# Recurrence and gated feed-forward on one core: two inputs turned by DMA transposes, and a new order for the first 900 jobs

## Chip, cores and metric

One core of a Trainium2 chip runs the whole program. The metric is device time in microseconds (us); smaller is better. TensorE (PE) does matrix products and turns tiles with an identity matrix, VectorE (DVE), ScalarE (ACT) and GpSimd (POOL) work element by element, and SyncE (SP) issues the DMAs, one queue for all of them.

## The reference

Four sequences of 5824 tokens with 256 channels pass a gated linear recurrence, and then a feed-forward block that multiplies two projections. In short:

```python
a_base = 1 / (1 + exp(-a_param))                  # [256]
a_t = exp(8 * sigmoid(r_gate) * log(clip(a_base)))
x_gated = sqrt(max(1 - a_t*a_t, 1e-6)) * sigmoid(i_gate) * x
for t in range(S):
    h = a_t[:, t] * h + x_gated[:, t]             # the scan over time
    y[:, t] = h
tok = y.reshape(23296, 256)
out = ((tok @ w1) * (tok @ w2)) @ w3 @ w_out      # 256 -> 1024 -> 1024 -> 256
```

## The kernel before

The 23296 tokens are cut into 47 chunks: chunks 0 and 1 have 256 tokens, chunks 2 to 45 have 512, chunk 46 has 256. Chunks 0 and 1 share their tiles up to the scan. Since nothing stands between the last two products, w3 and w_out are first folded into one 1024 x 256 matrix `wp_sb`, in eight pieces.

The program is a list of small jobs. Each is a letter with a chunk number and further indices, and one long string, `ORDER`, gives their sequence; each engine works through its own jobs in that sequence and waits wherever an input or a free buffer is missing. For a chunk c the jobs are:

- `r`, `i`, `x`: loads of r_gate, i_gate and x, tokens on the partitions. `Lw..` and `Cw..` load a piece of a weight and cast it to bf16.
- `R`, `I` (ACT): tanh of half the gates. `p` (POOL) adds 1 to the i gate. `t` multiplies it with x into `u_t`, in two halves, on POOL, or on DVE for the entries of `DV_HALF`.
- `V` turns `th_r`, and `U` turns `u_t`, from tokens on partitions to channels on partitions. For chunks in `TURN_R` or `TURN_U` this is done by `turn_pe`: eight 128x128 transposes on PE into a PSUM tile `ptr`. For the others `turn_dma` issues one DMA transpose on SP into a tile `rt` or `ut`.
- `d` (ACT) takes the exponential: `a_t`. `s` squares it into `nrm` (POOL, or ACT for `AC_SQUARE`, DVE for `DV_SQUARE`), `q` (ACT) takes the square root, `g` (DVE) multiplies by the turned `u_t`, `h` (DVE) scans, one instruction for each half of the channels, `y` casts the result to bf16 (POOL unless named elsewhere). A tile `y_t` is what PE needs to begin on a chunk.
- `a` and `b` (PE) are the projections by w1 into `pa` and by w2 into `pb`; `c` copies `pa` out of PSUM into `sa` (ACT, or DVE for `DV_COPY`), `m` (DVE) multiplies `sa` by `pb` into `g_t`.
- `D` (PE) multiplies `g_t` by `wp_sb` into `po`, `e` evacuates it into `ot` (ACT, or DVE for `DV_EVAC`), `o` stores.
- `Ft`, `Fc`, `Fm`, `Fe` fold w3 with w_out: PE transposes into `ptw`, a copy into `w3t`, PE products into `pw`, a scaled copy into `wp_sb`.
- `W` (PE) are products of the identity with itself. They compute nothing; they stand where PE would have nothing else to do at the start.

The tiles `ptr`, `pa`, `po`, `ptw` and `pw` share one ring of four PSUM buffers, taken in the order of the program; `pb` and the tiles of `W` share a ring of two. So a `pa` can be written only when the fourth tile before it has been read. `u_t` has two buffers, `ut` six.

A chunk in both `TURN_R` and `TURN_U` is loaded in long rows: each partition takes four neighbouring tokens, 4 KB in one piece, and the later jobs reorder them. Any other chunk is loaded with 1 KB rows. The two ways of turning, and that rule, are:

```python
def long_rows(c):
    return c in TURN_R and c in TURN_U

def turn_pe(c, key, nm, half=None):            # shortened: one matmul for each 128x128 block
    nc.tensor.matmul(out=pt[:, cb - cbs[0], j * P:(j + 1) * P],
                     lhsT=flat(T[nm, c])[:, j, cb * P:(cb + 1) * P], rhs=ident, is_transpose=True, ...)

def turn_dma(c, key, nm):
    ...
    nc.sync.dma_start_transpose(out=dense(dst, n).rearrange("p cb j q -> p (cb j) q"),
                                in_=dense(T[nm, c], n).rearrange("p cb j q -> p (cb j q)"))
```

The line numbers in the rows below: 155 load, 196 product into `u_t`, 204 PE turn, 215 DMA transpose, 227 exponential, 235 and 237 square, 242 root, 252 and 255 the product `g`, 274 scan, 284 and 286 cast to `y_t`, 291 `W`, 303 projections, 324 and 326 PSUM copies, 341 product `m`, 361 down product, 418 and 420 weight casts, 429 and 440 folding products, 474 and 476 the scaled copy. In the changed kernel each number is two lower.

## Time and profile before

| | |
|---|---|
| median of 3 runs | 510.43 us (510.37 to 511.27) |
| the profiled execution | 510.6 us, of which 508.8 us from the first to the last instruction |
| PE busy | 497.0 us, 98% |
| DVE, ACT, POOL busy | 445.7, 452.2, 299.9 us |
| DMA moved | 124.32 MB, mean 244 GB/s |

Busy time says that an instruction was in progress. Matmuls overlap one another, so the pace of PE is read from the starts of neighbouring rows, and whether it stands still from the waits.

### The profile page before, as it was taken

How to read it: one execution, taken by the hardware profiler on the slowest of the kernel's cores; microseconds unless marked ns; L12 is line 12 of the kernel's file. 1: busy time of each engine (PE TensorE's matmuls, PEld its weight loads, DVE VectorE, ACT ScalarE, POOL GpSimd, SP SyncE). 2: the span in 40 equal slices, each digit the busy share in tenths (PEclk: the TensorE clock that was granted, in tenths of full speed). 3: DMA queues.
4: the chain of work that ended last, by engine and by line, in shares of the span. 5: the costliest groups of instructions: out<-in, count | busy, mean ns of one | idle time of the engine just before them, and what ended most of it. 6: DMA issues, size and time to landing. Idle time of an engine off the chain costs nothing.

```text
span 508.8 us, 8833 instructions
## 1 busy us (share of the span) xinstructions
PE 497.0 (98%) x3162; PEld 307.4 (60%) x3217; DVE 445.7 (88%) x450; ACT 452.2 (89%) x683; POOL 299.9 (59%) x261
## 2 busy tenths in 40 slices
...
GB/s 319 399 369 338 261 270 330 289 268 273 310 294 272 241 274 283 321 266 293 242 278 337 252 268 195 220 238 227 208 248 152 240 316 146 89 167 62 64 52 104
DMA packets 179104, 124.32 MB, mean 244 GB/s; under 512 B 88434, under 2 KB 175092, under 8 KB 179060
## 3 DMA queue, kind: packets, MB, share of 16 engines
...
## 4 chain that ended last, share of the span: by engine, by line
PE 85%; ACT 6%; DMA 3%; issue 3%; DVE 2%; POOL 1%; SPq 0%; DVEq 0%; ACTq 0%; POOLq 0%
PE po L361 28%; PE pb L303 27%; PE pa L303 26%; ACT sa L326 2%; DMA x_t<-in_x_dram 2%; PE pw L440 1%; ACT a_t L227 1%; DMA i_t<-in_i_gate_dram 1%; PE ptr L204 1%; DVE h_t L274 1%; ACT ot L326 1%; PE ptw L429 1%; ACT L172 1%; ACT nrm L242 0%; ACT th_r L166 0%
## 5 line engine op out<-in xcount | busy, mean ns | idle before, releaser
L341 DVE TENSOR_TENSOR g_t<-sa,pb 128x1024 bf16<-128x1024 bf16 (+1 forms) x188 | 217.9, 1178 | 44.4 <-PE pb L303 21.6
L303 PEld LDWEIGHTS <-w_sb 128*128 128x128 bf16 x1504 | 146.4, 98 | 146.0 <-POOL w_sb L420 1.6
L326 ACT CAST sa<-pa 128x512 bf16<-128x512 f32 (+1 forms) x311 | 168.8, 587 | 35.4 <-PE pa L303 24.4
L303 PE MATMUL pb<-y_t,w_sb 128*128 128x512 bf16 (+1 forms) x737 | 182.8, 372 | 2.7 <-DVE g_t L341 1.6
L303 PE MATMUL pa<-y_t,w_sb 128*128 128x512 bf16 (+1 forms) x712 | 183.5, 372 | 1.4 <-ACT sa L326 0.2
L361 PE MATMUL po<-wp_sb,g_t 128*128 128x256 bf16 (+1 forms) x1464 | 176.6, 272 | 0.6
L361 PEld LDWEIGHTS <-g_t 128*128 128x128 bf16 x1464 | 142.6, 98 | 38.4
L286 POOL CAST y_t<-h_t 128x1024 bf16<-128x1024 f32 (+2 forms) x45 | 47.3, 1052 | 166.4 <-DVE h_t L274 157.7
L274 DVE TENSOR_TENSOR_SCAN h_t<-a_t,h_t,nrm 128x512 f32<-128x512 f32 (+1 forms) x92 | 116.1, 1294 | 1.5
L196 POOL TENSOR_TENSOR u_t<-i_t,x_t 128x512 bf16<-128x512 f32 (+1 forms) x83 | 113.8, 1385 | 1.7 <-DMA ut<-u_t 0.7
L237 POOL TENSOR_TENSOR nrm<-a_t 128x512 f32<-128x512 f32 (+1 forms) x69 | 74.3, 1091 | 12.4 <-ACT a_t L227 12.3
L227 ACT ACTIVATE a_t<-rt,la 128x512 f32<-128x512 bf16 (+1 forms) x82 | 65.9, 819 | 0.1
L177 POOL TENSOR_SCALAR i_t<-i_t 128x1024 f32<-128x1024 f32 (+1 forms) x45 | 55.2, 1229 | 5.2 <-ACT i_t L172 5.2
L255 DVE SCALAR_TENSOR_TENSOR nrm<-nrm,ut 128x1024 f32<-128x1024 f32 (+1 forms) x40 | 52.9, 1325 | 4.0 <-ACT nrm L242 4.0
L326 ACT COPY ot<-po 128x512 f32<-128x512 f32 (+1 forms) x75 | 43.7, 584 | 13.1 <-PE po L361 12.8
L242 ACT ACTIVATE nrm<-nrm 128x1024 f32<-128x1024 f32 (+1 forms) x47 | 48.5, 1039 | 0.4
L172 ACT ACTIVATE i_t<-i_t 128x1024 f32<-128x1024 f32 (+1 forms) x46 | 48.5, 1058 | 0.1
L166 ACT ACTIVATE th_r<-r_t 128x1024 bf16<-128x1024 f32 (+1 forms) x41 | 43.3, 1056 | 0.0
L324 DVE CAST sa<-pa 128x512 bf16<-128x512 f32 x57 | 37.9, 683 | 1.4 <-PE pa L303 0.5
L242 ACT ACT_TABLE_LOAD x17 | 21.8, 1283 | 0.4
L235 ACT ACTIVATE nrm<-a_t 128x512 f32<-128x512 f32 x22 | 13.9, 635 | 0.1
L324 DVE COPY ot<-po 128x512 f32<-128x512 f32 (+2 forms) x18 | 11.5, 646 | 2.2 <-PE po L361 2.1
...
## 6 DMA issues: line engine op xcount, KB each, us to landing
...
wf<-in_moe_w_out_dram SPq DMA_DIRECT2D x2, 512.0 KB, 11.1
rt<-th_r SPq DMA_TRANSPOSE x41, 4.3
ut<-u_t SPq DMA_TRANSPOSE x40, 4.1
```

The source lines that it names most:

```text
L172: nc.scalar.activation(out=t[:, :n, :], in_=t[:, :n, :], func=AF.Tanh, scale=0.5)
L177: (nc.vector if c in DV_PLUS else nc.gpsimd).tensor_scalar(t, t, 1.0, 1.0, op0=ALU.add, op1=ALU.mult)
L196: (nc.vector if (c, half) in DV_HALF else nc.gpsimd).tensor_mul(out=u, in0=t, in1=xt)
L227: nc.scalar.activation(out=a, in_=pr, func=AF.Exp, scale=la4[:, cb:cb + 1], bias=la4[:, cb:cb + 1])
L237: (nc.vector if (c, cb) in DV_SQUARE else nc.gpsimd).tensor_mul(out=n, in0=a, in1=a)
L242: nc.scalar.activation(out=n, in_=n, func=AF.Sqrt, scale=-1.0, bias=1.0)
L255: nc.vector.scalar_tensor_tensor(out=n, in0=n, scalar=1e-3, in1=T["pu", c][:, :, cols], op0=ALU.max, op1=ALU.mult)
L274: nc.vector.tensor_tensor_scan(h[:, cb, :], a[:, cb, :], n[:, cb, :], init, ALU.mult, ALU.add)
L303: nc.tensor.matmul(out=dst, lhsT=w_sb[:, cb, m * P:(m + 1) * P], rhs=T["y", gates_of(c)][:, cb, span(c, mp)], start=(cb == 0), stop=(cb == ...
L326: nc.scalar.copy(out=dst, in_=src_ps)
L341: nc.vector.tensor_mul(out=T["g", z][:, 2 * mp:2 * mp + 2, span(c, mp)], in0=T["sa", c, mp][:, :, :w], in1=T["pb", c, mp][:, :, :w])
L361: nc.tensor.matmul(out=po, lhsT=T["g", c][:, k, j * P:(j + 1) * P], rhs=wp_sb[:, k, cols], start=(k == 0), stop=(k == KD - 1), skip_group_ ...
```

## The change

`TURN_U` loses chunks 5 and 7: their `u_t` is turned by a DMA transpose into `ut` and no longer by eight PE transposes into `ptr`. Chunk 7 was in both lists and so was loaded in long rows; now its three loads have 1 KB rows. The tables that say which engine does a copy, square, cast or half product are rewritten for chunks 0 to 19 or so, and the string `ORDER` is new up to its 900th job, in chunk 18; from there on it is the same word for word. The number of `W` jobs (16) is unchanged.

```diff
-    TURN_U = {0, 2, 3, 4, 5, 7}
+    TURN_U = {0, 2, 3, 4}
-    DV_HALF = {(2, 0), (10, 0), (14, 0), (15, 1), (18, 0), (27, 0), (28, 0)}
-    DV_SQUARE = {(0, 0)}
+    DV_HALF = {(5, 0), (5, 1), (10, 0), (27, 0), (28, 0)}
+    DV_SQUARE = {(0, 0), (13, 0)}
-    DV_CAST = {(0, 0), (1, 0)}
+    DV_CAST = {(1, 1)}
-    FOLD_ACT = {('c', 4), ('e', 0), ('e', 3), ('e', 5), ('e', 6)}
+    FOLD_ACT = {('c', 2), ('e', 0), ('e', 1), ('e', 2), ('e', 3), ('e', 5), ('e', 7)}
-    W_ACT = {('w1', 1)}
-    W_DVE = set()
+    W_ACT = {('w3', 3), ('w3', 5)}
+    W_DVE = {('w1', 0), ('w2', 0), ('wo', 0)}
...
-        E A3. r0 W5 A0. A1. A2. R0.0 W1 R0.1 W9 V0.0 i0 d0.0 s0.0 V0.1 d0.1 s0.1 x0 W7 I0 t0.1 t0.0 r2 W4 W3 W15
+        E r0 A3. A0. A1. W9 W1 W5 R0.0 V0.0 R0.1 V0.1 A2. d0.0 s0.0 x0 d0.1 s0.1 W12 i0 I0 W7 t0.1 t0.0 W14
```

Counted over the program, 16 PE transposes and two PSUM tiles go, and two DMA transposes come (83 in place of 81). DVE loses five of its `e` copies and two of its half products and gains three weight casts; ACT gains those five copies and two casts of pieces of w3, and loses the cast of a piece of w1 and four squares.

The first place is VectorE from the two products for chunks 0 and 1 (`u_t`) to the scan of chunk 2 (the last two `h_t` rows). Before:

```order
L193 SCALAR_TENSOR_TENSOR u_t<-i_t,x_t 128x512 x2
L252 SCALAR_TENSOR_TENSOR nrm<-nrm,ptr 128x256 x2
L274 SCALAR_TENSOR_TENSOR h_t<-a_t,nrm 128x256 x2
L286 CAST y_t<-h_t 128x256
...
L324 CAST sa<-pa 128x2x256
L341 TENSOR_TENSOR g_t<-sa,pb 128x2x256 x2
L196 TENSOR_TENSOR u_t<-i_t,x_t 128x512
...
L252 SCALAR_TENSOR_TENSOR nrm<-nrm,ptr 128x512 x2
L274 SCALAR_TENSOR_TENSOR h_t<-a_t,h_t,nrm 128x512 x2
```

and now, on the same engine over the same stretch:

```order
L191 SCALAR_TENSOR_TENSOR u_t<-i_t,x_t 128x512 x2
L418 CAST w_sb<-wf 128x2x512
L250 SCALAR_TENSOR_TENSOR nrm<-nrm,ptr 128x256 x4
...
L272 SCALAR_TENSOR_TENSOR h_t<-a_t,h_t,nrm 128x256
L418 CAST w_sb<-wf 128x2x512
L322 CAST sa<-pa 128x2x256 x2
...
L250 SCALAR_TENSOR_TENSOR nrm<-nrm,ptr 128x512 x2
L272 SCALAR_TENSOR_TENSOR h_t<-a_t,h_t,nrm 128x512
L418 CAST wo_sb<-wf 128x1024
L272 SCALAR_TENSOR_TENSOR h_t<-a_t,h_t,nrm 128x512
```

Three weight casts have come in, the last between the two halves of the scan, and the half product into `u_t` of chunk 2 has gone to POOL.

The second place is ScalarE from the exponential of chunk 2 (`a_t` from `ptr_224`, now `ptr_214`) to the copies `sa<-pa` of chunks 0 and 1. Before:

```order
L227 ACTIVATE a_t_235<-ptr_224,la4_85 128x512 x2
L326 CAST sa_246<-pa_240 128x2x256
L418 CAST w1_sb_90<-wf_251 128x2x512
L235 ACTIVATE nrm_285<-a_t_235 128x512
L242 ACT_TABLE_LOAD
L242 ACTIVATE nrm_285<-nrm_285 128x1024
L326 CAST sa_309<-pa_302 128x2x256
L164 ACT_TABLE_LOAD
L164 ACTIVATE th_r_311<-r_t_307 128x1024
L326 CAST sa_360<-pa_355 128x2x256
L227 ACTIVATE a_t_394<-ptr_377,la4_85 128x512 x2
```

and now:

```order
L233 ACTIVATE nrm_263<-a_t_237 128x512
L162 ACTIVATE th_r_311<-r_t_229 128x1024
...
L240 ACTIVATE nrm_263<-nrm_263 128x1024
L225 ACT_TABLE_LOAD
L225 ACTIVATE a_t_343<-ptr_334,la4_85 128x512 x2
L324 CAST sa_354<-pa_349 128x2x256
L324 COPY w3t_365<-ptw_356 128x1024
L324 CAST sa_397<-pa_371 128x2x256
L162 ACTIVATE th_r_401<-r_t_367 128x1024
L324 CAST sa_403<-pa_374 128x2x256
L472 ACTIVATE wp_sb_93<-pw_405 128x256
L324 CAST sa_419<-pa_384 128x2x256
```

The tanh of chunk 3 (`th_r_311`) now stands ahead of the root of chunk 2 (`nrm_263` from itself), and four copies of `pa`, one of `w3t` and one into `wp_sb` follow the exponential of chunk 3 (`a_t_343`).

The third place is SyncE around the new transpose of chunk 5 (`ut_935<-u_t_787`), and VectorE from the second half of that `u_t` to the product that reads the result. SyncE before, where the first transpose of a `u_t` stands (that of chunk 6):

```order
L155 DMA r_t_919<-in_r_gate_dram 128x4x256
L155 DMA x_t_935<-in_x_dram 128x1024
L215 DMA_TRANSPOSE rt_951<-th_r_949 128x8x128
L155 DMA i_t_966<-in_i_gate_dram 128x4x256
L215 DMA_TRANSPOSE ut_1001<-u_t_946 128x8x128
```

SyncE now:

```order
L213 DMA_TRANSPOSE rt_857<-th_r_813 128x8x128
L153 DMA x_t_881<-in_x_dram 128x4x256
L153 DMA i_t_895<-in_i_gate_dram 128x4x256
L213 DMA_TRANSPOSE ut_935<-u_t_787 128x8x128
L382 DMA out_0_dram<-ot_845 128x2x256
L382 DMA out_0_dram<-ot_905 128x2x256
L213 DMA_TRANSPOSE rt_987<-th_r_852 128x8x128
```

VectorE now:

```order
L194 TENSOR_TENSOR u_t_787<-i_t_759,x_t_785 128x2x2x128
L322 CAST sa_879<-pa_876 128x512
L339 TENSOR_TENSOR g_t_718<-sa_818,pb_864 128x1024
L322 COPY ot_905<-po_883 128x512
L322 CAST sa_879<-pa_910 128x512
L322 CAST sa_929<-pa_922 128x512
L322 CAST sa_874<-pa_925 128x512
L339 TENSOR_TENSOR g_t_946<-sa_874,pb_916 128x1024
L322 CAST sa_948<-pa_931 128x512
L253 SCALAR_TENSOR_TENSOR nrm_892<-nrm_892,ut_935 128x1024
```

Chunk 5's `u_t` is now made on VectorE, its transpose stands in SyncE's queue ahead of two stores and of the transpose `rt_987` of chunk 8, and eight VectorE instructions lie between the half product and the reader of the result.

## Rows read from the trace of the kernel before

**Rows 1.** Page, part 1: busy us (share) and instructions.

```profile
PE 497.0 (98%) x3162; PEld 307.4 (60%) x3217; DVE 445.7 (88%) x450; ACT 452.2 (89%) x683; POOL 299.9 (59%) x261
```

**Rows 2.** Windows: PE, PEld, DVE, ACT, POOL busy (instructions); PEclk, DMA, GB/s.

```profile
27.00:75.00 48.00, 47.60 (x362) 31.85 (x368) 46.66 (x58) 44.09 (x62) 32.58 (x31) 1.00 1.08 310
75.00:250.00 175.00, 173.95 (x1053) 104.81 (x1072) 171.70 (x173) 166.02 (x245) 110.37 (x93) 1.00 1.05 284
```

**Rows 3.** Waits of PE, 27 to 509 us: total, times, longest.

```profile
PE pa L303 <- ACT sa L326: 0.2, 1, 0.2
```

**Rows 4.** Waits of ACT, 27 to 75 us, first and last of six.

```profile
ACT sa L326 <- PE pa L303: 1.5, 3, 0.7
...
ACT a_t L227 <- PE ptr L204: 0.2, 1, 0.2
```

**Rows 5.** Chain that ended last: start us, us, what.

```profile
5.80 11.34 DMA x_t<-in_x_dram
...
28.35 1.73 PE pa L303 x8
...
33.59 0.88 PE pw L440 x8
```

**Rows 6.** Timeline of PE at chunk 5's turn: start us, us, what.

```profile
60.60 0.61 PE L204 MATMUL ptr<-ident,u_t 128*128 128x128 bf16 x8
61.05 1.15 PE L361 MATMUL po<-wp_sb,g_t 128*128 128x256 bf16 x9
```

**Rows 7.** Timeline of PE: first product on chunk 2.

```profile
26.90 0.38 PE L303 MATMUL pa<-y_t,w_sb 128*128 128x512 bf16 x1
```

**Rows 8.** Timeline of DVE and POOL, 10 to 27 us.

```profile
10.28 0.75 DVE L252 SCALAR_TENSOR_TENSOR nrm<-nrm,ptr 128x256 f32<-128x256 f32 x2 [0.79 <-PE ptr L204]
11.07 1.27 DVE L274 TENSOR_TENSOR_SCAN h_t<-a_t,nrm 128x256 f32<-128x256 f32 x2
12.38 0.30 DVE L286 CAST y_t<-h_t 128x256 bf16<-128x256 f32 x1
...
18.46 1.27 DVE L324 CAST sa<-pa 128x512 bf16<-128x512 f32 x2
19.52 1.27 POOL L196 TENSOR_TENSOR u_t<-i_t,x_t 128x512 bf16<-128x512 f32 x1
...
22.05 1.27 DVE L252 SCALAR_TENSOR_TENSOR nrm<-nrm,ptr 128x512 f32<-128x512 f32 x2
23.25 2.50 DVE L274 TENSOR_TENSOR_SCAN h_t<-a_t,h_t,nrm 128x512 f32<-128x512 f32 x2
25.81 1.04 POOL L286 CAST y_t<-h_t 128x1024 bf16<-128x1024 f32 x1 [2.31 <-DVE h_t L274]
```

**Rows 9.** Timeline of ACT, 13 to 26 us.

```profile
17.57 1.28 ACT L242 ACT_TABLE_LOAD   x1
18.87 1.06 ACT L242 ACTIVATE nrm<-nrm 128x1024 f32<-128x1024 f32 x1
...
23.48 1.45 ACT L227 ACTIVATE a_t<-ptr,la 128x512 f32<-128x512 bf16 x2 [0.24 <-PE ptr L204]
24.82 1.05 ACT L164 ACTIVATE th_r<-r_t 128x1024 bf16<-128x1024 f32 x1
```

**Rows 10.** Tiles `ut`, then `rt`, 0 to 120 us: DMA transposes from issue to landing.

```profile
DMA to landing us min/median/max: 3.5/4.6/5.0
DMA to landing us min/median/max: 4.3/5.5/8.1
```

**Rows 11.** Groups by form: count, busy us, mean ns, idle before.

```profile
L341 DVE TENSOR_TENSOR g_t<-sa,pb 128x1024 bf16<-128x1024 bf16 x176 | 209.9, 1212 | 39.0 <-PE pb L303 20.5 <-ACT sa L326 10.4 <-ACT a_t L227 2.3
...
L326 ACT CAST sa<-pa 128x512 bf16<-128x512 f32 x303 | 166.1, 593 | 30.2 <-PE pa L303 20.4 <-DVE g_t L341 7.1 <-PE pw L440 1.0
...
L474 ACT ACTIVATE wp_sb<-pw 128x256 bf16<-128x256 f32 x4 | 1.5, 374 | 0.3 <-PE pw L440 0.3
...
L326 ACT COPY w3t<-ptw 128x1024 bf16<-128x1024 bf16 x1 | 1.0, 1018 | 0.0
```

More of the change, by code (lines that the diff above doesn't have):

```diff
@@ new lines @@
+        s2.0 c0.0.0 t2.1 b0.1 m0.1 a1.1.1 c1.1.0 Lw3.2 Cw3.2 Lw1.1 Cw1.1 b0.0 m0.0 a1.0.0 a1.0.1 c1.0.0 b1.1
+        m1.1 b1.0 m1.0 R3 Lwo.1 Cwo.1 s2.1 U2 q2 g2 W8 h2.0 V3 d3.0 d3.1 Lwo.0 Cwo.0 a0.2.1 a0.2.0 c0.2.0 Ft2
+        Fc2 r4 Lw3.0 a1.3.1 a1.2.0 a1.3.0 h2.1 y2 a1.2.1 a0.3.1 b0.2 b1.3 c1.3.0 m0.2 m1.3 R4 c1.2.0 Fm2 Fe2
+        Cw3.0 a0.3.0 c0.3.0 V4 b0.3 a2.0.1 m0.3 s3.0 c2.0.1 a2.0.0 d4.0 c2.0.0 d4.1 Lw3.1 Cw3.1 i3 I3 s4.0 b1.2
+        m1.2 s4.1 Ft0 Lw3.5 b2.0 Cw3.5 s3.1 Fc0 a2.2.1 c2.2.1 a2.1.0 Ft1 m2.0 c2.1.0 Fm0 Fc1 Fe0 b2.1 q3 a2.1.1
@@ new lines @@
+        d5.1 V6 a3.1.0 c3.1.0 t5.1 b3.1 d5.0 a4.3.1 s7.1 c4.3.1 a4.1.0 c4.1.0 x8 D0.3 s5.1 m3.1 i8 D0.2 e0.1
+        d6.0 s5.0 a4.1.1 c4.1.1 s6.0 b4.3 I7 a4.0.1 a4.3.0 d6.1 c4.0.1 a4.2.1 q5 U5 a4.0.0 q7 t6.0 c4.0.0 o0.0
+        s6.1 c4.3.0 m4.3 c4.2.1 g5 h5.0 q6 p7 b4.1 o0.1 D2.1 D2.0 h5.1 y5 e2.0 a4.2.0 m4.1 V8 D2.2 b4.0 D3.1
+        d8.1 D3.0 e3.0 I8 D2.3 c4.2.0 e2.1 b4.2 m4.0 m4.2 a5.1.0 d8.0 x7 c5.1.0 a5.3.1 c5.3.1 t7.1 r9 t7.0 U6
+        r10 R10 o2.0 a5.0.0 c5.0.0 i9 a5.3.0 c5.3.0 g6 h6.1 h6.0 y6 b5.3 p8 t8.0 a5.1.1 m5.3 D3.2 D3.3 r11
@@ new lines @@
+        c7.0.0 V12 x11 t9.0 U9 o4.0 o4.1 r13 i12 h8.0 a7.2.0 h8.1 c7.2.0 a7.3.1 c7.3.1 m7.3 b7.2 q10 s9.0 m7.2
+        s9.1 q9 g9 h9.1 D6.2 D6.3 e6.1 I11 D5.1 D5.0 e5.0 y8 a8.2.0 c8.2.0 d12.0 a8.2.1 c8.2.1 i14 h9.0 V11
+        d12.1 R13 D5.3 D5.2 e5.1 a8.1.0 c8.1.0 i13 b7.0 m7.0 t10.1 U10 a8.1.1 r14 o6.1 c8.1.1 a8.0.1 b8.2 m8.2
+        V13 a8.0.0 c8.0.1 c8.0.0 y9 a9.1.1 c9.1.1 o5.0 o5.1 b8.0 p11 m8.0 I12 d11.0 a9.1.0 t11.0 t11.1 d11.1 x13
+        s11.1 c9.1.0 b8.1 m8.1 g10 h10.0 a9.0.0 c9.0.0 I13 b9.1 a9.2.1 h10.1 D6.0 p13 D6.1 a9.2.0 e6.0 c9.2.0
@@ new lines @@
+        m9.1 U11 a9.0.1 c9.2.1 c9.0.1 x12 r16 b9.0 R15 a8.3.1 D7.3 c8.3.1 R14 m9.0 s12.1 V15 i15 d13.0 a8.3.0
+        s11.0 d13.1 b9.2 D7.2 e7.1 D7.0 b8.3 q11 D7.1 y10 a10.0.1 e7.0 s13.0 p12 a10.0.0 c10.0.1 c10.0.0 o6.0
+        m9.2 c8.3.0 m8.3 g11 a10.3.0 c10.3.0 o7.1 a10.1.1 c10.1.1 a10.1.0 c10.1.0 h11.0 h11.1 a10.3.1 c10.3.1
+        V14 b10.0 b10.3 t13.1 m10.0 d15.0 t13.0 R16 m10.3 a9.3.1 d15.1 r17 c9.3.1 i16 U13 D8.1 y11 D8.0 e8.0
+        t12.1 I14 d14.0 a10.2.0 t12.0 p14 s13.1 a10.2.1 b10.1 m10.1 c10.2.1 b10.2 c10.2.0 x14 V16 D8.3 m10.2
```

111 lines of the change are left out of this document (45 added, 66 removed), and 11 rows, old and new, of the table DV_COPY.

## The prediction

> **What bounds the kernel now.** I read the page's busy times first. PE is busy 98% of the span, DVE and ACT 88% and 89% [rows 1]. Busy time alone proves nothing for PE, because its matmuls overlap, so I went to the waits and the pace. From 27 us to the end PE waits for another engine once, for 0.2 us [rows 3]. In the chain that ended last, eight products of 512 columns take 1.73 us, 0.216 each, and eight of 256 columns take 0.88, 0.109 each [rows 5]: no gaps at all. So from 27 us on the time is PE's own work, and only two things can shorten it: less work, or an earlier start. The reader should also see how little room the helpers have: between 75 and 250 us DVE is busy 171.7 of 175 us and ACT 166.0 [rows 2]. PE runs freely, but only because both just keep up.
>
> Before 27 us PE is mostly waiting. Its first product on chunk 2 starts at 26.90 [rows 7]. In the order, real PE work ahead of that product is 48 turns (0.056 each, since the eight of chunk 5 start 0.45 before the next row [rows 6]), 64 half-chunk products of 256 columns and one piece of the folding (eight turns and eight such products): 2.7 + 7.0 + 0.4 + 0.9 = 11.0 us. The other 15.9 us are `W` and idle time. What ends them is `y_t` of chunk 2, cast by POOL from 25.81 to 26.85 after DVE's scan ended at 25.75 [rows 8].
>
> **The two turns removed.** Eight transposes occupy PE for 61.05 - 60.60 = 0.45 us [rows 6], and chunk 7's set has the same eight instructions. Two sets are 0.90 us. They stand where PE never waits, so this comes off the end, unless something new makes PE wait: -0.90.
>
> **The two transposes added.** A DMA transpose of a `u_t` lands 3.5 to 5.0 us after its issue in the first 120 us, median 4.6, and of a `th_r` up to 8.1 [rows 10]. For chunk 5 the cover is DVE itself: between the half product and the product that reads `ut` stand eight instructions, six of the 0.6 us kind (two 512-column copies take 1.27, and they overlap [rows 8]) and two products of 1.2 [rows 11]: 5.9 us or so. Median and worst of `ut` fit under it, so I cost it at nothing; an 8.1 us landing would stall DVE 2.2 us. Behind it on SP wait two stores and the turn of chunk 8, none of them due at once. Chunk 7's `u_t` is made long before its scan. Its loads in 1 KB rows are made early too; I cost them at nothing between bounds of 0 and a landing later by a few tenths.
>
> On this the Trainium skill speaks against the change: "VectorE: DVE Perf Modes", Rules for kernel authors, says to turn on TensorE where PSUM will do as the destination, and its table of three transpose paths gives 390 ns for a 128x128 tile there and 1309 by DMA. The rows agree on the direction, 0.45 us against 4.6 for a whole tile, but latency matters only where the cover ends; by that rule alone the sum would be the late-transpose case below.
>
> **The new start, by hand.** I follow two chains to the place where PE has done as much as it had at 26.90.
>
> DVE first. Before its row at 10.28 it stands idle for 0.79 us, until PE has turned the first `u_t` [rows 8]; one weight cast fits in that gap. No such cast on DVE is in the trace. The nearest row is a 256-wide one at 0.30 [rows 8]; four times that, 1.2, is the upper bound, and a 512-column copy at 0.6 the lower, being less data. I take 0.65, because part of the 0.30 is fixed cost.
>
> The page "VectorE: DVE Perf Modes", in its perf-mode tier table, gives 1227 ns for an fp32 copy of 2048 elements; an estimate for 1024 from that page is 0.7 us, and with it the sum would not move.
>
> Then four 256-wide products of 0.33 (two take 0.75 with their overlap), from 10.3 to 11.7; three scans of 0.64 (two take 1.27 [rows 8]) and a cast of 0.3, 13.9; the last scan, 14.6; the second weight cast, 15.2; four copies and four products at 0.6, 20.1. The product of chunk 2 needs the turned `u_t`. Its x is the tenth load on SP in both orders, and lands at 17.14 [rows 5]; the two halves are now both on POOL, 1.27 each [rows 8], so 19.7, the turn and its passage 20.4. From there 1.2 for the product, 1.25 for the first scan, 0.6 for the third weight cast, 1.25 for the second scan, 24.8; POOL's cast 1.04, 25.9. That is 0.9 us before the present time, as the half product on DVE that runs now and one `w3t` copy are gone from this stretch. With weight casts of 1.2 it would be 27.3.
>
> Now ACT. Ahead of the table load at 17.57 stand three instructions of much the same sum in both orders (copy, weight cast, square; now square, tanh, square), so the root still ends at 19.93 [rows 9]. The tanh of chunk 3 is done by then, so the exponential of chunk 3 follows a table load of 1.28 directly: 21.2 to 22.65, in place of 23.48 to 24.93 [rows 9]. After it come four copies of 0.59, a `w3t` copy of 1.02 and a scaling of 0.37 [rows 11], and a tanh of 1.05 [rows 9]: 4.8, less some 0.1 of overlap each (the exponential ends 0.11 after the next row starts [rows 9]), so 26.75, or 27.45 without overlap. The last of these copies frees the PSUM buffer for the second pair of chunk 2's products. Ahead of that pair PE has done what it had done at 26.90: four half-chunk products less (0.44), two of 512 columns more (0.43). So ACT sets the start at about 26.8 against 26.90: -0.1, with bounds of -0.5 (the `y_t` alone decided: 25.95, less the 0.44 that PE still owes) and +0.7 (no overlap, or slow casts).
>
> **After 27 us.** DVE loses five evacuations and ACT gains them; the other exchanges are in the diff. On ACT I count five copies of 0.59, two weight casts near 1.05 and two scalings of 0.37 more, one weight cast and four squares (like copies, an estimate) less: +2.4 us. ACT stands idle 48 - 44.1 = 3.9 us between 27 and 75 us [rows 2], and the six rows of its waits there all end on PE [rows 4]. It waits because it is ahead. I therefore let that idle time swallow the 2.4, and cost it at 0; if none were swallowed it is +2.4.
>
> **The sum.** The profiled execution took 510.6 us: 510.6 - 0.90 - 0.1 = 509.6. It was 0.17 above the median of the runs shown, 510.43, so on the median **509.4**.
>
> **The rivals.**
> - *A better start.* PE wastes 15.9 us ahead of chunk 2, so there is room. If x of chunk 2 lands some tenths sooner and ACT's copies overlap more, the start gains 1 in place of 0.1: 508.5. Against it: ACT's chain has no gap to close.
> - *Gain given back.* PE comes earlier by 0.9, and at the tight places of 27 to 250 us DVE or ACT is not earlier with it: PE waits what it had saved, 510.3. DVE's 98% speaks for it [rows 2]; its lost evacuations speak against it.
> - *ACT becomes the bound* (slower). The place is 27 to 75 us, where ACT has 3.9 us of idle time and gets 2.4 of work. If its idle time stays, because its inputs come in the wrong order, PE waits 2.4: 509.4 + 2.4 = 511.8. It decides from 2.0 us not swallowed (0.9 + 0.1 saved, and 1.0 for the bound of slower). Against it: [rows 4].
> - *The transposes come late* (slower): the rule above as a mechanism. With the 8.1 us landing of [rows 10] the product of chunk 5 is 2.2 us late, and if nothing takes it up PE waits so long for `y_t` of chunk 5: 509.4 + 2.2 = 511.6. It needs more than 5.9 us, which no `ut` row shows.
>
> **How the numbers follow.** A measurement of this kernel can tell about 0.2%, 1.0 us, from no change. The sum as worked out has 0.50, with its own range 508.9 to 510.0; its centre lies at that boundary, so I give 0.27 of it to faster and 0.23 to the same. The better start has 0.18, the gain given back 0.17, ACT as the bound 0.10, late transposes 0.05. Faster: 0.27 + 0.18 = 0.45. Same: 0.23 + 0.17 = 0.40. Slower: 0.15. The range reaches from 508.2 (start at the better bound with some tenths of [rows 3] and of other idle time) to 510.9; above it lies most of the slower cases, and below a little of the better start.
>
> **What would show it.** Right: the first product on chunk 2 near 26.2 and the second pair near 26.8; no waits of PE after 27 us beyond some tenths; the landing of chunk 5's `ut` under 5.9 us and no DVE wait for it; ACT's idle time between 27 and 75 us down to about 1.5 us. Wrong: a PE wait on `sa` or `ot` of ACT by the microsecond (ACT bound), a DVE wait on `ut` (late transposes), or a first product on chunk 2 after 27.5 (weight casts on DVE dearer than 0.65).

## The result, and the profile after

The changed kernel takes 511.59 us (median of 21 runs) against 510.55 for the kernel before (21 runs, taken in turn with it): ratio 1.0021, 95% interval 1.0015 to 1.0028. It is 1.0 us slower, where 509.4 was predicted with a range to 510.9. One of its 21 executions took 1365.8 us and is left out of the ratio. The profiled execution took 512.71 us, with a span of 510.9: 1.1 above the median, so a second one was profiled later (511.05 us, span 509.2, called the second profile here). The rows of both are needed, because they differ in just what matters.

A correction to the section on the change: the two orders differ up to their 1100th of 2449 words (chunk 18), not their 900th.

First the waits of PE from 27 us to the end (us in total, times, longest), here of the first profile. They answer to [rows 3].

```profile
PE pa L301 <- ACT sa L324: 1.2, 2, 1.0
PE pa L301 <- DVE ot L322: 0.6, 1, 0.6
```

The second profile has the first of these lines alone, with the same numbers. Before, there was 0.2 us, near 368 us, and the same 0.2 is in both sums. The timeline of PE says where the rest is: in the first profile at 170.5 and 220.9, in the second only at 219.2 (start us, us, what, and in brackets the idle time ahead and what ended it).

```profile
170.51 1.46 PE L301 MATMUL pa<-y_t,w_sb 128*128 128x512 bf16 x6 [0.62 <-DVE ot L322]
...
220.91 1.02 PE L301 MATMUL pa<-y_t,w_sb 128*128 128x512 bf16 x4 [1.00 <-ACT sa L324]
```

```profile
219.19 1.02 PE L301 MATMUL pa<-y_t,w_sb 128*128 128x512 bf16 x4 [1.03 <-ACT sa L324]
```

Start to start, less the pace of [rows 5], these and some smaller gaps are 2.6 us between 165 and 222 us in the first profile, and 1.2 in the second.

What is late there is VectorE. These are the scans (tile `h_t`) among VectorE's groups between 165 and 222 us (count, busy us, mean ns), before, in the first profile, and in the second:

```profile
L274 DVE TENSOR_TENSOR_SCAN h_t<-a_t,h_t,nrm 128x512 f32<-128x512 f32 x10 | 12.4, 1270 | 0.2
```

```profile
L272 DVE TENSOR_TENSOR_SCAN h_t<-a_t,h_t,nrm 128x512 f32<-128x512 f32 x10 | 15.8, 1600 | 0.3
```

```profile
L272 DVE TENSOR_TENSOR_SCAN h_t<-a_t,h_t,nrm 128x512 f32<-128x512 f32 x10 | 14.4, 1453 | 0.3
```

Ten scans each time, on tiles of the same size: 12.4, 15.8 and 14.4 us. The timeline of the first profile around one of them, VectorE and GpSimd:

```profile
167.72 2.16 DVE L272 TENSOR_TENSOR_SCAN h_t<-a_t,h_t,nrm 128x512 f32<-128x512 f32 x1
169.80 0.66 DVE L322 COPY ot<-po 128x512 f32<-128x512 f32 x1
...
167.76 1.05 POOL L175 TENSOR_SCALAR i_t<-i_t 128x1024 f32<-128x1024 f32 x1 [2.11 <-ACT i_t L170]
168.77 1.94 POOL L235 TENSOR_TENSOR nrm<-a_t 128x512 f32<-128x512 f32 x1
```

A GpSimd instruction runs from 167.76 to 168.81; the scan ends 1.07 us after that, at 169.88; the next GpSimd instruction, a square that takes 1.04 elsewhere, ends 0.83 after the scan, at 170.71. So it looks as if they take turns. The copy `ot` behind the scan comes at 169.80, and PE waits for it at 170.5. The same two instructions in the second profile:

```profile
167.39 1.28 DVE L272 TENSOR_TENSOR_SCAN h_t<-a_t,h_t,nrm 128x512 f32<-128x512 f32 x1
...
167.46 2.05 POOL L175 TENSOR_SCALAR i_t<-i_t 128x1024 f32<-128x1024 f32 x1 [2.14 <-ACT i_t L170]
```

There the scan's record begins 0.07 us ahead, where it was 0.04 in the first profile; the scan keeps its 1.28, and the GpSimd instruction takes 2.05 in place of 1.05. So it is GpSimd that waits, and PE does not stop at 170. In both profiles the two scans of chunk 20 are the long ones (2.09 and 2.12 at 212.69 and 215.81 in the first, 2.08 and 2.12 in the second), and the wait near 220 follows. The chain to it in the second profile is the second scan, the product `m` (`g_t`), ScalarE's copy, which waits for that product, and PE's 219.19 above:

```profile
214.09 2.12 DVE L272 TENSOR_TENSOR_SCAN h_t<-a_t,h_t,nrm 128x512 f32<-128x512 f32 x1
...
217.31 1.20 DVE L339 TENSOR_TENSOR g_t<-sa,pb 128x1024 bf16<-128x1024 bf16 x1
...
218.55 0.58 ACT L324 CAST sa<-pa 128x512 bf16<-128x512 f32 x1 [0.73 <-DVE g_t L339]
```

The products `g` (tile `nrm`), which also read two tiles of SBUF, are lengthened too, and more so before: five between 165 and 222 us take 7.2 us before, 6.3 in the first profile and 6.6 in the second. Scans and `g` together, VectorE has 2.5 and 1.4 us more to do there than before, which is about what PE loses.

The windows, to be set beside [rows 2] (PE, PEld, DVE, ACT, POOL busy, granted clock, DMA, GB/s; first profile):

```profile
27.00:75.00 48.00, 48.00 (x360) 31.73 (x359) 46.13 (x55) 46.19 (x66) 32.58 (x31) 1.00 1.04 327
75.00:250.00 175.00, 173.18 (x1061) 103.57 (x1060) 170.85 (x166) 164.18 (x240) 113.67 (x94) 1.00 1.04 277
```

Between 27 and 75 us PE is never idle, and ACT's idle time is down from 3.9 to 1.8 us. VectorE's busy time between 75 and 250 us is hardly changed, 170.85 after 171.70: a lengthened scan counts as busy, so the sum hides it.

The start. PE's first product on chunk 2 comes at 26.89 in the first profile and at 26.61 in the second; the second again, with VectorE's scans and weight cast and GpSimd's casts ahead of it:

```profile
26.61 1.02 PE L301 MATMUL pa<-y_t,w_sb 128*128 128x512 bf16 x4
...
21.53 2.15 DVE L272 TENSOR_TENSOR_SCAN h_t<-a_t,h_t,nrm 128x512 f32<-128x512 f32 x1
23.60 0.66 DVE L418 CAST wo_sb<-wf 128x1024 bf16<-128x1024 f32 x1
24.19 1.27 DVE L272 TENSOR_TENSOR_SCAN h_t<-a_t,h_t,nrm 128x512 f32<-128x512 f32 x1
...
21.56 1.04 POOL L418 CAST wo_sb<-wf 128x1024 bf16<-128x1024 f32 x1
25.52 1.04 POOL L284 CAST y_t<-h_t 128x1024 bf16<-128x1024 f32 x1 [2.92 <-DVE h_t L272]
```

The first scan of chunk 2 is long too, beside GpSimd's weight cast of 21.56 to 22.60, and `y_t`, which ends at 26.56, decides the start.

**A ledger.** To split the difference I take the time at which PE starts a product, less the work that the program has ahead of it (about 0.217 us for 512 columns, half for 256, 0.056 for a turn, `W` left out; the next digit of the pace shifts all three kernels alike). At 42 us this is 16.13 before, 16.34 in the first profile, 16.06 in the second; at 200 us 16.16, 17.50, 16.15; at 235 us 16.16, 19.10, 17.38; from there to the end all three lose 0.65 to 0.68. So in the second profile: -0.90 (the turns) - 0.07 (to 42 us) + 0.06 (to 200 us) + 1.23 (200 to 235) = +0.32, and its last 40 down products start at 502.44 against 502.11 before, +0.33. The first profile is another 1.75 later (504.19): 0.28 up to 42 us, where `la_rows`, the load of a_param on ACT's queue, lands at 3.0 in place of 2.1 us, and the rest in the longer waits at 165 to 222 us.

### The profile page after: what moved, and what is told of

It is laid out like the page before. It is cut to its first block, busy times and chain, and to the rows that moved or that the text cites. A ratio compares the mean times of both kernels' runs of the same rounds, so it can differ in the third digit from the quotient of the medians.

```text
span 510.9 us, 8867 instructions
## 1 busy us (share of the span) xinstructions
PE 500.0 (98%) x3201; PEld 307.4 (60%) x3201; DVE 446.8 (87%) x442; ACT 454.8 (89%) x688; POOL 304.5 (60%) x263
## 4 chain that ended last, share of the span: by engine, by line
PE 87%; DVE 3%; ACT 3%; DMA 3%; issue 1%; POOL 1%; SPq 0%; DVEq 0%; ACTq 0%; POOLq 0%
PE po L359 29%; PE pa L301 28%; PE pb L301 28%; DMA x_t<-in_x_dram 3%; DVE g_t L339 1%; PE pw L438 1%; ACT sa L324 1%; DVE h_t L272 1%; PE ptw L427 1%; ACT L240 1%; POOL u_t L194 0%; ACT nrm L240 0%; ACT ot L324 0%; PE ptr L202 0%; DVE ot L322 0%
## 5 line engine op out<-in xcount | busy, mean ns | idle before, releaser
L301 PE MATMUL pa<-y_t,w_sb 128*128 128x512 bf16 (+1 forms) x752 | 189.5, 372 | 2.6 <-ACT sa L324 1.2
L284 POOL CAST y_t<-h_t 128x1024 bf16<-128x1024 f32 (+2 forms) x46 | 49.0, 1066 | 154.7 <-DVE h_t L272 141.4
L272 DVE TENSOR_TENSOR_SCAN h_t<-a_t,h_t,nrm 128x512 f32<-128x512 f32 (+1 forms) x92 | 121.3, 1344 | 1.7
L194 POOL TENSOR_TENSOR u_t<-i_t,x_t 128x512 bf16<-128x512 f32 (+1 forms) x85 | 115.6, 1374 | 1.8 <-DMA ut<-u_t 0.7
L235 POOL TENSOR_TENSOR nrm<-a_t 128x512 f32<-128x512 f32 x72 | 80.2, 1128 | 11.5 <-ACT a_t L225 11.5
L324 ACT COPY ot<-po 128x512 f32<-128x512 f32 x80 | 46.7, 585 | 14.2 <-PE po L359 13.6
L253 DVE SCALAR_TENSOR_TENSOR nrm<-nrm,ut 128x1024 f32<-128x1024 f32 (+1 forms) x42 | 55.4, 1322 | 4.0 <-ACT nrm L240 4.0
L233 ACT ACTIVATE nrm<-a_t 128x512 f32<-128x512 f32 x18 | 11.2, 645 | 0.0
L322 DVE COPY ot<-po 128x512 f32<-128x512 f32 (+2 forms) x13 | 8.1, 624 | 2.0 <-PE po L359 2.0
```

Of the source, the lines that this page charges most:

```text
L194: (nc.vector if (c, half) in DV_HALF else nc.gpsimd).tensor_mul(out=u, in0=t, in1=xt)
L235: (nc.vector if (c, cb) in DV_SQUARE else nc.gpsimd).tensor_mul(out=n, in0=a, in1=a)
L253: nc.vector.scalar_tensor_tensor(out=n, in0=n, scalar=1e-3, in1=T["pu", c][:, :, cols], op0=ALU.max, op1=ALU.mult)
L272: nc.vector.tensor_tensor_scan(h[:, cb, :], a[:, cb, :], n[:, cb, :], init, ALU.mult, ALU.add)
L284: (nc.vector if key in DV_CAST else nc.gpsimd).tensor_copy(out=y, in_=h)
L301: nc.tensor.matmul(out=dst, lhsT=w_sb[:, cb, m * P:(m + 1) * P], rhs=T["y", gates_of(c)][:, cb, span(c, mp)], start=(cb == 0), stop=(cb == ...
```

## The experiments

Theories N and P are mine: the loss is made by the new order between 165 and 222 us (N), by scans that meet GpSimd instructions (P). The rivals stand in each expectation. In the diffs `NEW` and `OLD` are the two orders as lists of words; the table entries of a job go with the order it is taken from. Line numbers shift between these kernels, so read the tile names. Single waits of PE in the text are start to start, less the pace; the lists of waits give up to 0.2 us less for them and leave some out. The kernel before ran beside all of them, at 510.35 to 510.47.

**The turns alone, in the old order** (`U5` and `U7` gone from their old places).

```diff
-    TURN_U = {0, 2, 3, 4, 5, 7}
+    TURN_U = {0, 2, 3, 4}
...
-        t5.1 t5.0 r9
+        t5.1 t5.0 U5 r9
...
-        c5.3.0 I10 t7.0 a5.0.1
+        c5.3.0 I10 t7.0 U7 a5.0.1
```

> The old order and tables, with chunks 5 and 7 turned by DMA (their transposes issued right behind the second half product). Theory N (the loss comes with the new order between 165 and 222 us, the turns are worth what eight transposes of 0.45 us take): 510.5 - 0.9 = 509.6 us, and no wait of PE after 27 us above some tenths. Theory T (the DMA turns themselves cost what they save): 510.5 or more. Theory S (the new start costs 1 us): 509.6 too.

Measured: 517.3 us, ratio 1.0135 (1.0121 to 1.0149). That lies within theory T's "510.5 or more", but the turns had only 0.9 us to give back, and 7 us are lost. SyncE's queue (first fence) and ACT (second) show it:

```profile
57.06 1.24 SPq L207 DMA_TRANSPOSE ut<-u_t  x1
58.35 0.57 SPq L147 DMA_DIRECT2D r_t<-in_r_gate_dram  x1
```

```profile
62.73 1.06 ACT L158 ACTIVATE th_r<-r_t 128x1024 bf16<-128x1024 f32 x1 [5.43 <-DMA r_t<-in_r_gate_dram]
```

The transpose waits for its `u_t` until 57.06, and the load of r that stands behind it in the same queue goes out at 58.35; before, it went out at 48.68. ACT stands still for 5.43 us. PE then waits 3.2 us at 64.9 to 68.1, and its clock falls with it (the columns are as in the windows above):

```profile
64.90:68.10 3.20, 0.08 (x1) 0.00 (x0) 1.40 (x1) 3.19 (x5) 2.49 (x2) 0.90 1.11 380
68.10:71.50 3.40, 3.36 (x14) 1.85 (x14) 3.37 (x4) 3.37 (x4) 0.17 (x1) 0.59 1.16 281
71.50:75.00 3.50, 2.87 (x14) 1.18 (x13) 3.43 (x5) 3.33 (x7) 3.33 (x3) 1.00 1.14 221
```

After the idle stretch PE runs near the lower level (1.2 GHz) for 3 us and comes back. So what the added transpose costs here is the load that stands behind it.

**The turns in the old order, placed behind those loads.**

```diff
-        p6 a4.3.0 c4.3.0 x7 p7
+        p6 a4.3.0 c4.3.0 x7 U5 p7
...
-        y5 a5.1.0 c5.1.0 r11
+        y5 a5.1.0 c5.1.0 t7.1 t7.0 U7 r11
```

> The old order and tables, the two DMA turns again, but each transpose now stands on SyncE behind the loads that the first attempt had kept waiting (chunk 5's behind the load of x of chunk 7, chunk 7's between two loads, right behind its second half product). Theory Q (the transposes cost nothing themselves; the 7 us of the first attempt were loads queued on SyncE behind a transpose that waits for its u_t): 510.5 - 0.9 = 509.6 us, and PE without waits between 27 and 340 us. Theory T (the transposes themselves are late or in the way): 512 or more, with VectorE waiting for ut.

Measured: 512.3 us, ratio 1.0039 (1.0027 to 1.0050). 5 of the 7 us are gone. Theory Q's 509.6 did not come; it is theory T's number and sign, a wait of VectorE for `ut`. The waits between 60 and 90 us:

```profile
PE pa L295 <- POOL y_t L278: 1.2, 1, 1.2
DVE nrm L247 <- DMA ut<-u_t: 0.9, 1, 0.9
```

Here the rival of late transposes is real: chunk 5's transpose lands 0.9 us after VectorE wants it, `y_t` is late, and PE waits 1.2. In the new order the same transpose is issued at 54.89, VectorE's reader of it starts at 61.33, 6.4 us later, and does not wait. In neither of these two placements do the turns pay without the new order, so the two parts of the change are not priced apart.

**The new order alone, with the turns on PE.** Only `TURN_U` goes back, and each of `U5` and `U7` to just ahead of its `g`.

> The new order and tables, with chunks 5 and 7 turned on PE as before (each turn moved to just ahead of the product that reads it). Theory N: the changed kernel's 511.6 + 0.9 = 512.5 us, with the waits between 165 and 222 us still there. Theory T: 510.5. Theory S: 512.5, with the first product on chunk 2 late.

Measured: 514.0 us, 1.0075 (1.0062 to 1.0088). Of the 3.5 us over the kernel before, 1.3 are a wait at 79.4, where the turn `U7` now stands too late for its product (my placing); 2.2 are waits between 204 and 222 us. So the loss in the middle does not hang on the DMA turns.

**One order first, then the other.**

```diff
-    for word in NEW:
+    for word in NEW[:690] + [w for w in OLD if w not in NEW[:690]]:
```

> The first 690 jobs as in the changed kernel (to about 135 us, with its start and its two DMA turns), the rest in the old order with the old tables. Theory N: the waits of PE between 165 and 222 us (2.6 us) are gone: 511.6 - 2.6 = 509.0, or up to 510.0 if the join costs something. Theory S: 511.6, as the start is the new one. Theory T: 511.6.

Measured: 512.7 us. No wait of PE from 147 to 340 us, as theory N says, but 3.3 us of waits at the join (134 to 146), so it doesn't decide. The mirror image, `OLD` (with the turns as in the first experiment) for 702 words, then `NEW`:

> The first 702 jobs in the old order (to about 137 us, with chunks 5 and 7 turned by DMA as in the kernel above), the rest in the new order with the new tables. Theory N: 509.6 + 2.6 = 512.2 us, less what the earlier or later arrival at 165 us takes up: 511.2 to 512.2, with waits of PE between 165 and 222 us. Theory S: 509.6. Theory T: 511.6.

Measured: 523.5 us. It carries the 7 us of the first experiment, and 5.7 more in waits between 142 and 232 us. In kind for theory N, in size no test. The next one joins them at word 610, where the two have done the same jobs but for three:

> The first 610 jobs as in the changed kernel (to about 118 us), the rest in the old order with the old tables; at this place the two orders have done the same jobs but for three. Theory N (the loss is the new order between 165 and 222 us): no wait of PE above 0.3 us from 27 to 340 us, 509.3 us. If a gain of 1 us made before 118 us is simply given back later, whatever the order: waits of PE of 1 us between 165 and 222 us, 510.5.

Measured: 511.04 us, 1.0012 (1.0004 to 1.0021). No PE wait between 133 and 340 us, as theory N says; but there is a wait of 0.84 at 124.5, behind ACT, and theory N's 509.3 is missed by 1.7 us. By the ledger PE comes to 165 us 0.3 us later than in the kernel before, so this run does not exclude that an early PE is stopped there in any order (old_new_old2, below, comes 0.3 us early and is not stopped). I tried to mend that by moving the first square of chunk 13 off ACT:

> The kernel that follows the new order for 610 jobs and then the old one, with one more entry changed: the first square of chunk 13 goes from ScalarE to GpSimd, since at the join it stood ahead of a copy for which PE waited 0.84 us at 124.5. Theory N: that wait goes and no other comes: 511.0 - 0.8 = 510.2 us. If time gained ahead of 165 us is given back there whatever is done: 511.0.

Measured: 511.3 us, the wait unchanged (0.83). The square was on VectorE already, so this was the same kernel again, and the 0.27 us between its two medians shows what a difference between two sets of runs can be without a cause in the kernel. The instruction in the way was the second square of chunk 15.

**What GpSimd reads.** In the changed kernel, for chunks 17 to 23:

```diff
+        if c in BLIND:
+            nc.gpsimd.memset(t, 1.0)
+            return
         (nc.vector if c in DV_PLUS else nc.gpsimd).tensor_scalar(t, t, 1.0, 1.0, op0=ALU.add, op1=ALU.mult)
```

and likewise for GpSimd's squares and half products, so that these three steps are left out of the computation.

> The changed kernel, in which GpSimd's instructions for chunks 17 to 23 (the +1 of the i gate, its squares and half products) only fill their outputs with a constant and read nothing: those three steps are left out of the computation. Theory P: every scan between 165 and 222 us takes 1.25 to 1.3 us, the waits of PE there fall from 2.6 to under 0.5, and the time to 509.3. Theory L: the scans may shorten, but the waits of PE stay: 511.0 or more.

Measured: 510.36 us (ratio to the kernel before 0.9994, 0.9985 to 1.0002), 1.2 less than the changed kernel's 511.59 (0.9 less than the 511.2 of its later runs, below), with no PE wait over 0.1 us between 165 and 222 us. Theory P's 509.3 is missed by 1.1. VectorE and GpSimd at the same scan as above:

```profile
167.81 1.28 DVE L274 TENSOR_TENSOR_SCAN h_t<-a_t,h_t,nrm 128x512 f32<-128x512 f32 x1
...
167.85 0.95 POOL L171 MEMSET i_t<- 128x1024 f32 x1 [5.22 <-ACT i_t L165]
168.74 0.53 POOL L235 MEMSET nrm<- 128x512 f32 x1
```

The same two engines are busy at the same time, GpSimd starting 0.04 us after the scan in both kernels, and the scan takes 1.28 in place of 2.16. Beside fills the scan is not lengthened. The fills are also shorter than the steps in whose place they stand (0.95 and 0.53 us here, for 1.05 and 1.04), but in neither profile of the changed kernel does an engine wait for GpSimd between 165 and 222 us, so earlier outputs of GpSimd could not have helped there. The control is the kernel before with the same steps left out:

> A control: the kernel before with the same GpSimd steps (chunks 17 to 23) left out as in pool_blind, each filling its output with a constant. In the old order no scan between 165 and 222 us was long and PE did not wait there. Theory P (the gain of pool_blind is the removal of collisions): nothing to remove, 510.4 us. If a lighter GpSimd helps in any order: 510.0 or less.

Measured: 510.47 us, ratio 1.0003 (0.9994 to 1.0012). A lighter GpSimd is worth nothing in the old order, although five products `g` fall from 7.2 to 6.1 us with it. So what is gained in the new order comes from what GpSimd reads beside the scans, and a collision costs PE something only where VectorE has no time to spare. (The kernel before has long scans as well, 2.03 and 2.22 us at 295.5 and 298.7, and PE does not wait there.)

**The disputed cost by itself.** Behind the last store of the kernel before:

```diff
+    pool_squares()      # six GpSimd squares of 128x512
+    scans()             # six VectorE scans of 128x512
```

and the other pairs, apart from one another.

> The kernel before, and behind its last store six scans of 128x512 on VectorE by themselves, six GpSimd squares by themselves, both together, the scans beside GpSimd fills, the scans beside ScalarE squares, and products of one PSUM and one SBUF input beside GpSimd squares. Theory P: together the six scans and six squares take turns, 6 x 1.25 + 6 x 1.0 = 13.7 us from first to last; beside fills, beside ScalarE, and for the products nothing lengthens. Theory L: 7.5 us for each pair.

In order: scans alone, squares alone, both together, scans beside fills, scans beside ScalarE's squares, products of PSUM and SBUF beside GpSimd's squares (start us, us of the group):

```profile
508.42 7.92 DVE L645 TENSOR_TENSOR_SCAN h_t<-a_t,nrm 128x512 f32<-128x512 f32 x6
...
520.11 6.63 POOL L650 TENSOR_TENSOR nrm<-a_t 128x512 f32<-128x512 f32 x6
...
530.01 11.20 DVE L645 TENSOR_TENSOR_SCAN h_t<-a_t,nrm 128x512 f32<-128x512 f32 x6
530.65 11.39 POOL L650 TENSOR_TENSOR nrm<-a_t 128x512 f32<-128x512 f32 x6
...
545.31 7.92 DVE L645 TENSOR_TENSOR_SCAN h_t<-a_t,nrm 128x512 f32<-128x512 f32 x6
545.93 6.93 POOL L670 MEMSET nrm<- 128x512 f32 x12
...
555.89 7.90 ACT L674 ACTIVATE nrm<-a_t 128x512 f32<-128x512 f32 x12
...
556.36 7.92 DVE L645 TENSOR_TENSOR_SCAN h_t<-a_t,nrm 128x512 f32<-128x512 f32 x6
...
567.42 4.29 DVE L679 TENSOR_TENSOR g_t<-sa,pb 128x512 bf16<-128x512 bf16 x6
568.06 6.63 POOL L650 TENSOR_TENSOR nrm<-a_t 128x512 f32<-128x512 f32 x6
```

Together, scans and squares last from 530.01 to 542.04, 12.0 us, where side by side they would take 7.9 and one after the other 14.6. So they take turns for the most part; 2.5 us overlap (theory P said 13.7). Beside fills and beside ScalarE the scans keep their 7.92 to the hundredth, and the squares keep their 6.63 beside products with one input in PSUM (those products were not run alone). The Trainium skill states this in "SBUF — State Buffer", section "Who interferes with whom": a VectorE instruction with two SBUF inputs contends with a GpSimd instruction that reads SBUF, not with one that only writes it, and the port pair that they share is an exclusive lock. The trace agrees: 12.0 us beside squares, which read, and 7.92 beside fills, which only write.

**Scans in pairs.**

```diff
-        m18.2 t21.1 i24 I23 e16.0 a19.0.1 r26 h20.0 d25.1 D16.2 e16.1 c19.0.1 a18.3.1 b19.1 m19.1 t22.0 p23 D17.3 o15.1 a18.3.0 h20.1
+        m18.2 t21.1 i24 I23 e16.0 a19.0.1 r26 h20.0 h20.1 d25.1 D16.2 e16.1 c19.0.1 a18.3.1 b19.1 m19.1 t22.0 p23 D17.3 o15.1 a18.3.0
```

and so for chunks 16 and 19.

> The changed kernel with the second scan of chunks 16, 19 and 20 put right behind the first, as the old order has it; nothing else moves. Theory P (the scans that meet a GpSimd instruction take 1.6 to 2.2 us in place of 1.25, because each second scan starts apart and finds one running; this makes VectorE late): at most two of these six scans above 1.5 us, the waits of PE between 165 and 222 us down from 2.6 to under 1, 509.9 us. Theory L (VectorE and ScalarE have too much to do there by the new tables, wherever the scans stand): 511.6, with the waits in place.

Measured: 514.2 us, 1.0076 (1.0059 to 1.0093): worse, against both. The first scans of chunks 16, 19 and 20 are short now (1.27 to 1.29), but the second ones, started right behind them, meet GpSimd (1.99, 2.07, 1.99): three long scans, where theory P allowed two. And what stood between the two scans comes a whole scan later:

```profile
PE pa L295 <- DVE ot L316: 1.7, 1, 1.7
PE pa L295 <- DVE sa L316: 1.5, 1, 1.5
```

So pairing the scans does not take them out of GpSimd's way, and this run decides nothing between theories P and L.

**A collision put into the old order.**

```diff
+        if 12 <= c <= 20:
+            T["y", c] = ring(ypool, [P, NCB, CT], BF16, name="y_t", tag="y")
+            nc.gpsimd.tensor_copy(out=T["y", c], in_=n)
```

> The kernel before, with one GpSimd cast more behind each product g of chunks 12 to 20; it reads what g has written, so it starts when the first scan wants to (its result is overwritten by the y cast). Theory P: the first scans of these nine chunks take about 2.1 us in place of 1.28, VectorE gets some 7 us more work where it has 2 to 3 us to spare, and PE waits for it: 513 to 516 us. Theory L (what GpSimd does beside a scan is no matter): 510.5.

Measured: 521.4 us, 1.021. No fair test: of PE's waits, 6.5 us are for `y_t` from GpSimd, since the added cast waits for `g` at the head of GpSimd's in-order queue and keeps its other work back. Seven scans of these chunks became long (1.80 to 2.22), but only two of them were first ones, not nine.

**A mend at the collision, nothing left out.**

```diff
-        i24 I23 e16.0 a19.0.1 r26 h20.0 d25.1 D16.2 e16.1 c19.0.1 a18.3.1 b19.1 m19.1 t22.0 p23 D17.3 o15.1 a18.3.0 h20.1 x23 o16.0 c18.3.1 I24
+        i24 e16.0 a19.0.1 r26 h20.0 h20.1 d25.1 D16.2 e16.1 c19.0.1 a18.3.1 b19.1 m19.1 t22.0 D17.3 o15.1 a18.3.0 x23 o16.0 c18.3.1 I23 p23 I24
```

> The changed kernel with a mend at the one place where both of its profiles have long scans: the tanh of i of chunk 23 (and with it GpSimd's +1, which starts 0.03 us before the first scan of chunk 20) stands four ScalarE jobs later, and the second scan of chunk 20 right behind the first. Nothing is left out. Theory P: both scans of chunk 20 at 1.25 to 1.3 us, no wait of PE near 219 us, so 1.2 us less than the changed kernel in its usual runs: 511.1 - 1.2 = 509.9 us. If ScalarE and VectorE are at their limit there with or without the long scans: the wait moves by some us and stays, 511.1.

Measured: 511.17 us, 1.0017 (1.0008 to 1.0026): no gain. The two scans of chunk 20:

```profile
211.03 2.44 DVE L266 TENSOR_TENSOR_SCAN h_t<-a_t,h_t,nrm 128x512 f32<-128x512 f32 x2
```

They are short, and the wait near 219 falls from 1.2 to 0.4 us. But PE is then stopped at 229.5 (0.3) and 243.0 (0.4), at jobs where it did not wait in either profile of the changed kernel: 1.1 us in all, so the time is the 511.1 of the rival. The mend has moved GpSimd's work into the next product `g`:

```profile
222.60 2.14 DVE L247 SCALAR_TENSOR_TENSOR nrm<-nrm,ut 128x1024 f32<-128x1024 f32 x1
...
222.40 1.27 POOL L188 TENSOR_TENSOR u_t<-i_t,x_t 128x512 bf16<-128x512 f32 x1
```

In the second profile of the changed kernel this product takes 1.22 (at 223.41, with GpSimd done at 222.51). So VectorE, 0.8 us ahead when it starts `g`, is 0.1 behind at the scans that follow (224.78 against 224.66), while PE is still 0.8 us ahead. The collision made the wait at 219, and the wait at 229.5 comes where a new collision has used up what VectorE had gained. Whether the one at 243.0 comes from it too is not shown.

**Where the rest is.** pool_blind is at 510.4, and the sum without the waits is 509.4. Four runs look for the difference: a mix of the two orders (old, new from job 196 to 610, old again), the same with its joins mended, and two variants of pool_blind.

> As the kernel before this one, but with the first 195 jobs (to about 38 us, the start with its weight casts and loads) in the old order too; there the two orders have done the same jobs but for two. If the new start is worth the 0.1 us that the prediction gave it: 510.3. If the late landings of la_rows, seen in three of six profiles of the new start and in none of four of the old one, belong to the new start and cost 0.5 us on average: 509.7. Theory N for the rest: no wait of PE above 0.3 us between 40 and 340 us.

Measured: 511.4 us, 1.0020 (1.0011 to 1.0029), with waits of 0.81 and 0.84 at the two joins.

> The old order for 195 jobs, the new one to job 610, the old one from there, with both waits at the joins mended: V7 two PE jobs later, and the second square of chunk 15 on GpSimd in place of ScalarE, where it stood ahead of the copy for which PE waited 0.84 us at 124.9. The earlier try at this wait named a square that was already on VectorE and so moved nothing. If the waits at the joins (0.81 and 0.84) were all that old_new_old lost: 511.4 - 1.65 = 509.8 us. If PE, 0.9 us early, is stopped at the next tight place: 510.4.

Measured: 510.82 us, 1.0010 (1.0001 to 1.0019). The wait at 124.9 is down to 0.3; at 40.6 there is still one of 0.7, now for `g_t` of VectorE in place of the turn.

> pool_blind (the changed kernel with the GpSimd steps of chunks 17 to 23 left out) with the first 195 jobs in the old order; at the join the turn V7 stands two PE jobs later. Theory S2 (what pool_blind still lacks to 509.3, some 0.6 to 0.9 us, is lost in the new start): 509.6, with PE 0.4 us or more ahead of pool_blind at 64 us. If the rest is lost elsewhere, by less work of PE being filled with other waits: 510.4.

Measured: 510.51 us, 1.0003 (0.9994 to 1.0012), with a wait of 0.7 at the join (41.3).

> pool_blind with the first load of i ahead of the first load of x on SyncE, as in the old order; nothing else moves. If the late landing of la_rows (3.0 to 3.3 in place of 2.1 us in three of seven profiles of the new start) comes from that exchange: la_rows at 2.1, and most times at pool_blind's lower group, 509.7 us. If it comes by chance or from something else: 510.4, with both groups of times as in pool_blind.

Measured: 510.33 us, 1.0001 (0.9992 to 1.0010), as pool_blind. The exchange of the two loads changes nothing that can be measured. Its profiled execution, at 509.98 us, comes nearest to the sum at PE's end. The last 40 down products of PE, in the kernel before and in this one:

```profile
502.11 3.68 PE L361 MATMUL po<-wp_sb,g_t 128*128 128x256 bf16 x40
```

```profile
501.25 3.68 PE L361 MATMUL po<-wp_sb,g_t 128*128 128x256 bf16 x40
```

0.86 us earlier: the 0.90 of the turns, with `la_rows` at 2.1 and no wait in the middle. So with GpSimd's reads gone PE runs through 165 to 222 us 0.9 us early and is not stopped: an early PE alone is not what makes the loss there. The time is only 0.6 less than in the profile before, since the rest is lost behind PE: the span ends 6.7 us after the start of these products in the kernel before and 6.9 in this one (7.0 in pool_blind, 7.05 in old_new_old2). Why the end takes longer there is not shown. Most of the other executions of blind_i_first take 0.3 us longer, and no profile shows those.

Last, the changed kernel once more, which gave the second profile shown above:

> The changed kernel once more, unchanged, for a second profile of it: the first was of an execution 1.1 us above the median, with la_rows late. If the waits of PE between 165 and 222 us belong to the order: again long scans of chunks 16, 19 and 20 and 1.2 to 2.6 us of waits there, whatever the start does. If they hang on a late start: with la_rows at 2.1 us they are under 0.5.

Measured: 511.2 us (8 runs, 510.07 to 512.15). The wait near 219 us belongs to the order: with `la_rows` at 2.1 it is there all the same. Those at 170 and 205 us are not there, so their scans were held up by GpSimd in one execution and not in the other.

## Why the prediction was wrong

- *The two turns, -0.90: right.* The ledger needs it, and blind_i_first shows 0.86.
- *The two transposes added, 0: right in this order.* VectorE does not wait for either. The cover for chunk 5 was 6.4 us from issue to reader (predicted 5.9; the traces have no landing for it); chunk 7's landed after 5.7 us in the first profile and 6.6 in the second, so 5.9 would not have been safe for every `ut`. How thin the cover is, turns_placed shows, where the same transpose cost 1.2 us of PE's time; there the rule of the Trainium skill that the prediction weighed ("VectorE: DVE Perf Modes", Rules for kernel authors: turn on TensorE) is borne out, here not. What I left out was SyncE's queue: in turns_only its price is 7 us, with loads behind a waiting transpose. That the new order avoids this I had shown and not priced.
- *The start, -0.1: near the number in the second profile (-0.07 at 42 us), but by luck, and late in the first.* At the first product on chunk 2 the second profile is not ahead: it starts at 26.61 (predicted near 26.2) with 10.51 us of PE's work behind it, where before it was 26.90 with 10.95, which leaves 16.10 against 15.95, 0.15 us worse. The rest comes from a place that the prediction did not have. In the old order a weight load waits for `w3t`, which [rows 3] does not list, and PE loses 0.18 us; the new order has no such wait:

```profile
40.61 0.44 PEld L440 LDWEIGHTS <-w3t 128*128 128x128 bf16 x5 [0.52 <-DVE w3t L324]
```

ACT's chain came as worked out (exponential of chunk 3 at 21.31, predicted 21.2; last copy out at 26.83, predicted 26.75), and the weight casts on VectorE took 0.66 to 0.68, predicted 0.65. The `y_t` of chunk 2 was predicted for 25.9 and ended at 26.56, because the first scan took 2.15 beside GpSimd's weight cast and not 1.25: the same collision, unseen, and so `y_t` set the start and not ACT. (The bounds -0.5 and +0.7 of this term give 509.0 to 510.2, not the 508.9 to 510.0 of the prediction; nothing hangs on it.) The first profile's late `la_rows` was seen in 3 of 10 profiles of kernels with the new start and in none of 10 with the old one; whether that is chance stays open.
- *ACT as the bound: it did not come.* As the sum had it, ACT's idle time between 27 and 75 us fell to 1.8 (predicted 1.5), and PE did not wait there.
- ***After 27 us*, "cost it at 0": the step that failed.** I asked of ACT's exchanges whether its idle time could swallow them and took the rest as neutral, from sums of busy time. The loss came from which instructions run side by side: between 165 and 222 us VectorE's ten scans take 14.4 or 15.8 us in place of 12.4, VectorE has no such time to spare (55.7 of 57 us busy there before), and PE waits 1.2 to 2.6 us. In other words, the prediction took the lengths of VectorE's instructions from the old trace and let the new order keep them. pool_blind with its control shows that what GpSimd reads in chunks 17 to 23 makes the loss, and side_by_side by how much the two engines lengthen each other. The rival *gain given back* had the place and the engine, but capped the loss at the 0.9 saved.

So in a usual execution: -0.90 - 0.07 + 0.06 + 1.23 = +0.32 to PE's end, +0.45 in time (511.05 against 510.6 in the profiles), and in some executions 1 to 2 us more; the medians differ by 1.0. That the mended orders did not come below 510.3 in the median, although the turns save 0.9, I can explain only in part: in old_new_old, old_new_old2, blind_old_start and i23_later PE was stopped at another place (0.3 to 0.85 us each), in pool_blind's profile `la_rows` came late (3.3), and in some 0.2 to 0.3 us were lost behind PE. No version here beats the kernel before.
